# Seven products instead of eight in the last two groups' second products, with a new beginning and a new written order

## The chip, the cores and the metric

The kernel runs on one core of a Trainium2 chip. The metric is the device time of one execution in microseconds (us). TensorE (PE) does the matrix products, VectorE (DVE), ScalarE (ACT) and GpSimd (POOL) the elementwise work, and SyncE (SP) issues nearly all transfers. Each engine takes its instructions in the order in which they stand in its own queue, and waits at one until its semaphores are there.

## The reference

An attention with a decaying state, a gated layer pair and a second layer pair, one behind the other, on 2 x 768 tokens (1536 rows of 512 features):

```python
for t in range(S):                      # per batch and head, D = 64, 8 heads
    state = gamma * state + outer(k[t], v[t])
    y[t] = scale * q[t] @ state
x  = y.reshape(1536, 512)
xn = x / sqrt(mean(x * x, -1) + 1e-06) * rms_g
x2 = (silu(xn @ w_gate) * (xn @ w_val)) @ w_out        # d_ff 1536
h  = x2 @ w_in                                         # d_ff 2048
out = maximum(0.01 * h, h) @ w_out2
```

## The kernel before

The attention runs over 12 chunks of 128 tokens. Its steps have short names in a written order (`ORDER`): `sc` scores, `ds` their decay by the mask (DVE), `kd` decayed keys (DVE for the chunks in `KD`, else ACT), `ou` outer products and `up` the new state, `yi` and `he` the two parts of the output, `sq`, `fa`, `sa`, `to`, `me`, `rs`, `sp`, `xs` the norm, `hi` and `lo` the two parts of the normed rows. Tokens with a colon convert a weight: the weights come as 64-bit numbers (tiles `raw_*`, 512 KB each), ACT and DVE turn one into a float32 tile `wa_*` (`P`, `1` to `4`) and split it into a high and a low part (`H` on ACT, `L` on DVE, tile `w_*`). `M`, `N`, `C` are the first gate and value products. Everything up to `Cv12` stands in this order; behind it, a planner writes the steps and a scheduler sets each engine's order.

Every product is made of three: high by high, high by low, low by high. A step of it is a matmul of 128 x 128 by 128 x 512. The tokens stand in three blocks of 512. The hidden columns come in pieces f of 128: g, v and o are gate, value and output of the first pair of layers (12 pieces, groups of 4, the names of their sums begin with `ao`), i and p input and output of the second (16 pieces, four groups, sums `ap`, kept in `y2acc`). For two pieces and the blocks 1 and 2, the products i (and g, v) are made as seven half products of sums instead of eight (`quad`, steps p1 to p7 into banks X, Y, Z); that takes sums of weights (tiles `w_s*`: four additions on 128 x 256 and two splits on DVE, two on ACT for a pair of pieces) and sums of the rows (`th`, `tl`). Block 0 is made plainly (`whole`).

The second products (`down`, L556) are plain in all blocks: for each piece and block the activated piece is split (`upper`, ACT, tile `gp_*h`; `lower`, DVE L571, tile `gp_*l`), and 12 matmuls add it into four PSUM banks. For p the split activation is the stationary operand and the weight the moving one, so the rows of a bank are tokens. When the four pieces of a group are through, `evac2` adds the four banks to `y2acc` (DVE L633), and in the last group stores them, 128 rows of 2 KB at a time. The last to be stored is block 2.

Seven matmuls on zeros (`warm`) begin PE's work. The small tables are issued by ACT, the rest by SP, in the order of `LOADS` (q, k a chunk's two transfers of 512 KB, m the mask, d the decay of q, w a weight). Transfers share eight completion semaphores in turn (`DMAHW0` to `DMAHW7` in the rows of the order below); one that takes up a semaphore waits for the transfer that had it before.

Of the kernel before, what the change touches and what calls it, by code (L numbers as in the profile page):

```python
# [13 lines left out]
ALU = mybir.AluOpType  # L14
# [10 lines left out]
HOLD = 2  # L25
# [33 lines left out]
def chain_kernel(ctx: ExitStack, tc: tile.TileContext, qk_t, kv, w1, w2, mask, qdec, kdec, sdec, rms_g, ident, out):  # L59
# [18 lines left out]
    scr = ctx.enter_context(tc.tile_pool(name="scr", bufs=5))  # L78
# [16 lines left out]
    expo = const.tile([P, 2], F32, name="expo")  # L95
    state = [const.tile([P, NPAIR, D], F32, name=f"state{i}") for i in range(4)]
# [16 lines left out]
    n_loaded = [0]  # L113

    def load(*items):
        for what in items:
# [6 lines left out]
            elif n == "d":  # L123
                nc.sync.dma_start(out=qdec_sb, in_=qdec)
# [213 lines left out]

    wq = []
    for kinds, fs in groups:  # L340
        for f in fs[::2]:
            for n in kinds:
                wq += [source(n, f), source(n, f + 1)]
                if n in TWICE and f"{n}{f}" not in PLAIN:
                    wq.append((f"s{n}{f}", None))
# [25 lines left out]
    def open_unit():  # L371
# [12 lines left out]
        if src is None:  # L384
# [9 lines left out]
            one, two = slice(0, 2 * P), slice(2 * P, 4 * P)  # L394
# [14 lines left out]

            return key, None, {  # L410
# [171 lines left out]
    def down(gi, f, b):  # L582
# [6 lines left out]
        if b == NB - 1:  # L589
            free(f"{L}{f}")  # L590
# [474 lines left out]
```

## Time and profile before

| | before |
|---|---|
| median of 3 runs | 598.89 us (598.23 to 599.38) |
| the profiled execution | 598.3 us |
| its span | 596.5 us |
| PE, DVE, ACT busy in the span | 583.4, 445.8, 334.2 us |
| mean granted PE clock | 0.994 |

The profile is of one execution; what lies outside its span is 598.3 - 596.5 = 1.8 us. Busy times of PE are modelled: matmuls overlap, so the time from one to the next is read from the chain, and not from the mean duration of one.

### The profile page before, as it was taken

Reading aid. Unit: us, or ns where it says so; the run is one execution under the profiler, and the core shown is the slowest. Engines: PE = TensorE matmul, PEld = TensorE weight load, DVE = VectorE, ACT = ScalarE, POOL = GpSimd, SP = SyncE. Lnnn points to the kernel's source line nnn. Section 1 sums busy time; section 2 is a strip of 40 time slices with the busy share of each in tenths; the row PEclk is TensorE's granted clock in tenths of the full one; section 3 lists DMA queues with packets and bytes.
Section 4 is the critical chain, followed back from the end, with each engine's and each line's share of the span. In section 5 each row is a group of like instructions: output and inputs, shape, how many; then the busy total and the mean of one; then the engine's idle time right before and its main releaser. Section 6 shows DMA issues by size and latency. Waiting matters only on the chain.

```text
span 596.5 us, 8244 instructions
## 1 busy us (share of the span) xinstructions
PE 583.4 (98%) x3147; PEld 482.5 (81%) x3147; DVE 445.8 (75%) x789; ACT 334.2 (56%) x612; POOL 20.7 (3%) x20
## 2 busy tenths in 40 slices
PE   6988999999999999999999999999999999999997
PEld 4977788888888888888888888878888888888885
DVE  3899999998578599599589989875767884631243
ACT  1679756776555465465474666776645474323320
POOL 0442100000000000000000000000000000000000
PEclk8999999999999999999999999999999999999999
DMA  8992321444122223123130211322312210000013
GB/s 301 410 372 73 106 73 35 142 111 128 45 70 72 71 71 88 54 70 110 67 107 0 96 48 35 107 70 73 105 36 70 71 36 1 0 2 0 1 70 141
DMA packets 16310, 52.76 MB, mean 88 GB/s; under 512 B 2448, under 2 KB 2576, under 8 KB 16272
## 3 DMA queue, kind: packets, MB, share of 16 engines
q1 hardware_dynamic: 15408, 52.17, 26.0%
q8 instruction: 24, 0.39, 0.3%
q10 hardware_dynamic: 864, 0.08, 0.1%
q14 instruction: 14, 0.11, 0.1%
HBM read 49.10 MB, written 3.15 MB: 88 GB/s over the span
## 4 chain that ended last, share of the span: by engine, by line
PE 93%; DVE 4%; DMA 2%; issue 1%; ACT 1%; ACTq 0%
PE ap L556 21%; PE ao L556 16%; PE g L526 7%; PE v L526 7%; PE i L526 7%; PE iX L753 7%; PE gX L753 5%; PE vX L753 5%; PE iZ L753 4%; PE gZ L753 2%; PE vZ L753 2%; PE iY L753 2%; PE sc L175 2%; PE y L236 1%; PE vY L753 1%; PE gY L753 1%
## 5 line engine op out<-in xcount | busy, mean ns | idle before, releaser
L556 PE MATMUL ap<-w_p,gp_1h 128*128 128x512 f32 x128 | 39.4, 389 | 0.0
L556 PE MATMUL ap<-w_p,gp_0h 128*128 128x512 f32 x128 | 39.4, 389 | 0.0
L556 PE MATMUL ap<-w_p,gp_2h 128*128 128x512 f32 x128 | 39.4, 389 | 0.0
L571 DVE TENSOR_TENSOR gp_0l<-i,gp_0h 128x512 fp32r<-128x512 f32 x16 | 11.0, 688 | 32.4 <-ACT gp_0h L564 32.4
L526 PE MATMUL g<-xh,w_g 128*128 128x512 f32 x128 | 32.4, 393 | 0.0
L526 PE MATMUL v<-xh,w_v 128*128 128x512 f32 x128 | 31.8, 390 | 0.0
L526 PE MATMUL i<-x2h,w_i 128*128 128x512 f32 x128 | 31.6, 389 | 0.0
L556 PE MATMUL ao<-go_2h,w_o 128*128 128x512 f32 x96 | 31.5, 389 | 0.0
L556 PE MATMUL ao<-go_0h,w_o 128*128 128x512 f32 x96 | 31.5, 389 | 0.0
L633 DVE TENSOR_TENSOR y2acc<-ap,y2acc 128x512 f32<-128x512 f32 x36 | 23.3, 685 | 10.4 <-PE ap L556 10.4
L556 PE MATMUL ao<-go_1h,w_o 128*128 128x512 f32 x96 | 30.5, 389 | 0.0
L526 PEld LDWEIGHTS g<-xh,w_g 128*128 128x128 f32 x128 | 23.7, 188 | 5.5 <-DVE hold L704 0.2
L556 PEld LDWEIGHTS ap<-w_p,gp_0h 128*128 128x128 f32 x128 | 24.0, 188 | 5.0
L556 PEld LDWEIGHTS ap<-w_p,gp_2h 128*128 128x128 f32 x128 | 24.0, 188 | 5.0
L526 PEld LDWEIGHTS i<-x2h,w_i 128*128 128x128 f32 x128 | 24.0, 188 | 5.0
L556 PEld LDWEIGHTS ap<-w_p,gp_1h 128*128 128x128 f32 x128 | 24.0, 188 | 5.0
L526 PEld LDWEIGHTS v<-xh,w_v 128*128 128x128 f32 x128 | 24.0, 188 | 4.9
L556 PE MATMUL ap<-w_p,gp_1l 128*128 128x512 f32 x64 | 25.1, 391 | 0.2 <-DVE gp_1l L571 0.2
L556 PE MATMUL ap<-w_p,gp_0l 128*128 128x512 f32 x64 | 24.9, 389 | 0.0
L556 PE MATMUL ap<-w_p,gp_2l 128*128 128x512 f32 x64 | 24.9, 389 | 0.0
L571 DVE TENSOR_TENSOR gp_2l<-hold,gp_2h 128x512 fp32r<-128x512 f32 x16 | 11.0, 688 | 16.4 <-ACT gp_2h L564 12.4
L564 ACT ACTIVATE gp_2h<-hold 128x512 fp32r<-128x512 f32 x16 | 10.1, 631 | 20.2 <-PE ap L556 20.2
(243 smaller groups left out, 1568.4 us busy)
## 6 DMA issues: line engine op xcount, KB each, us to landing
raw_i<-in_w SPq DMA_DIRECT2D x16, 512.0 KB, 3.7
raw_p<-in_w SPq DMA_DIRECT2D x16, 512.0 KB, 3.7
raw_g<-in_w SPq DMA_DIRECT2D x12, 512.0 KB, 3.6
raw_v<-in_w SPq DMA_DIRECT2D x12, 512.0 KB, 3.7
raw_o<-in_w SPq DMA_DIRECT2D x12, 512.0 KB, 3.6
qkT<-in_qk_t SPq DMA_DIRECT2D x7, 512.0 KB, 8.8
kv<-in_kv SPq DMA_DIRECT2D x7, 512.0 KB, 8.0
out<-y2acc SPq DMA_DIRECT2D x12, 256.0 KB, 2.1
```

Source lines behind the costliest of these rows:

```text
L175: nc.tensor.matmul(out=s["sc"][:, j, a, :], lhsT=k_[r, t], rhs=q_[r, t], start=True, stop=True)
L236: nc.tensor.matmul(out=s["y"][j * D:(j + 1) * D, a * CH:(a + 1) * CH], lhsT=s["kv"][:, 1, e:e + D], rhs=s["a"][:, j, a, :], start=not c % CPB,
L526: nc.tensor.matmul(out=dst, lhsT=lhs, rhs=rhs, start=(n == 0), stop=(n == len(pairs) - 1), skip_group_check=True)
L556: nc.tensor.matmul(out=acc["b"][m], lhsT=lhs, rhs=rhs, start=(start and n == 0), stop=(stop and n == 2))
L564: nc.scalar.activation(out=h, in_=x, func=AF.Copy)
L571: nc.vector.tensor_tensor(out=l, in0=x, in1=h.bitcast(F32), op=ALU.subtract)
L633: nc.vector.tensor_tensor(out=dst, in0=banks[m], in1=dst, op=ALU.add)
L753: nc.tensor.matmul(out=dst, lhsT=lhs, rhs=rhs, start=(start and n == 0), stop=(n == 5), skip_group_check=True)
```

## The change

The last two groups (`SEVEN = 2`) make their second products by seven half products as well. For a pair of pieces, sums of the weights p are formed (`w_sp*`), and sums of the activated pieces of blocks 1 and 2 one behind the other in place (`follow`); each of the seven (`seventh`, key q, numbers 1, 5, 6, 3, 7, 2, 4) is split by `upper` and `lower` like a piece, and goes in 6 matmuls into two banks X or Z. After each of the seven the two banks are added to a part of `y2acc`, while X goes on to gather. Both pairs of a group go through one number before the next; the plain products i of block 0 stand between. In these groups all four i are converted ahead of the p, and block 0's second products follow in the next group, or at the end.

For this the blocks 1 and 2 of all four groups now have features in the rows of a bank: the weight is the stationary operand, read with every second column (`by_quarter`). At the end DVE turns them back in squares of 32 (`transpose`), and 16 transfers of 32 partitions x 16 x 64 numbers store them, in runs of 256 B. Block 0 stays as it was and is stored last.

The beginning: ACT issues one table only, SP the others between the chunks; `turn` is no longer loaded in two broadcasts but made by two small matmuls (`across`). The table of ACT's functions is loaded by a first activation on a constant. Four more matmuls on zeros (`wm1`) stand ahead of `he0`, which now is ahead of `sc1`. `kd1` and `kd2` go to DVE, `kd4` to ACT. The written order is new throughout; a pool of scratch tiles has nine in place of five and two `hold` tiles.

```diff
-HOLD = 2
+SCRATCH = 9
+SEVEN = 2
-LOADS = "q0 k0 m q1 k1 q2 d k2 k3 q3 q4 q5 k4 w w q6 q7 k6 w k8 k7 k5 q8 q9 k9 q10 k10"
+LOADS = "q0 k0 m g s k1 q1 d q2 q3 k2 k3 q4 k4 q5 w w q6 w q7 k6 k8 k7 k5 i q8 q9 k9 q10 k10"
-KD = (0, 3, 4, 6, 7)
+KD = (0, 1, 2, 3, 6, 7)
-sc0 kd0 ts tk ou0 ds0 up0 sc1 kd1 he0 load ds1 sq0 ou1 qs1 xg0 sc2 up1 fa0 kd2 yi1 qs2 ds2 kd3 he1 sa0 qs3 ou2 sq1 sc3
+sc0 kd0 ou0 ds0 tb ts wm1 tk he0 load kd1 up0 sc1 sq0 qs1 xg0 ou1 ds1 qs2 sc2 up1 fa0 yi1 qs3 ds2 he1 kd2 sa0 ou2 kd3
...
+    def keep_warm(c, n=WARM):
+        s = ch.setdefault(c, {})
+        s["sc"] = ps_sc.tile([P, 2, NPAIR, CH], F32, tag="sc", name=f"sc{c}")
+        for _ in range(n):
+            nc.tensor.matmul(out=s["sc"][:, 0], lhsT=warm[:, :P], rhs=warm, start=True, stop=True)
...
+    def by_quarter(w, m):
+        return w.rearrange("p (h c m) -> p h m c", h=2, m=2)[:, m // 2, m % 2]
...
-                terms = (w[:, 0, part], h), (w[:, 0, part], l), (w[:, 1, part], h)
+                wh, wl = (w[:, i, part] if L == "o" else by_quarter(w[:, i, :], m) for i in range(2))
+                terms = (wh, h), (wh, l), (wl, h)
...
-        accumulate(L, gi, f, b, f == fs[0], f == fs[-1], L == "o")
+        accumulate(L, gi, f, b, f == fs[0], f == fs[-1], L == "o" or b > 0)
...
+    def follow(f, n):
+        t = turns[f]
...
+        if n == 1:
+            less(t[0, 1], t[0, 2], t[0, 1])
+            made["q", f, 5] = t[0, 1]
...
+    def seventh(gi, n, f):
...
+        upper(key)
+        lower(key)
+        h, l = parted.pop(key)
+        unit, half, side, start, (b, row) = SIDES[n]
...
+        for m in range(2):
+            wh, wl = (by_quarter(w[:, i, :], 2 * half + m) for i in range(2))
+            for k, (lhs, rhs) in enumerate(((wh, h), (wh, l), (wl, h))):
+                nc.tensor.matmul(
+                    out=acc[side][m],
...
+        for m in range(2):
+            dst = y2[b][:, 2 * row + m, :]
+            nc.vector.tensor_tensor(out=dst, in0=acc[side][m], in1=dst, op=ALU.add)
+        if gi == len(groups) - 1 and LAST[b, row] == n:
+            t = units.tile([P, 16, 32, 2], F32, tag="u", name=f"turned{b}_{row}")
+            for m in range(2):
+                nc.vector.transpose(
...
+            for i in range(4):
+                o = 2 * row * P + i * 64
+                nc.sync.dma_start(
+                    out=out[offs[b]:offs[b] + 512, o:o + 64].rearrange("(j r) d -> r j d", r=32),
+                    in_=t[32 * i:32 * i + 32].rearrange("p j c m -> p j (c m)"),
+                )
```

Three places of the order, before and after. A name's first number is its chunk, piece or group; the last one is a running number. First SP, from the start of the program, before:

```order
L132 DMA qkT0_114<-in_qk_t 128x1024
L134 DMA kv0_115<-in_kv 128x1024
L122 DMA mask_sb_91<-in_mask 128x512 [waits DMAHW0_49]
L122 DMA mask_sb_91<-in_mask 128x512 [waits DMAHW1_49]
L132 DMA qkT1_120<-in_qk_t 128x1024 [waits DMAHW2_49]
L134 DMA kv1_121<-in_kv 128x1024 [waits DMAHW3_49]
L132 DMA qkT2_124<-in_qk_t 128x1024 [waits DMAHW4_49]
L124 DMA qdec_sb_92<-in_qdec 128x512 [waits DMAHW5_49]
L134 DMA kv2_125<-in_kv 128x1024 [waits DMAHW6_49]
```

and of the change:

```order
L135 DMA qkT0_115<-in_qk_t 128x1024
L137 DMA kv0_116<-in_kv 128x1024
L125 DMA mask_sb_91<-in_mask 128x512 x2
L127 DMA g_sb_96<-in_rms_g 128x4
L127 DMA sdecs_94<-in_sdec 128x4
L137 DMA kv1_124<-in_kv 128x1024
L135 DMA qkT1_123<-in_qk_t 128x1024 [waits DMAHW0_49]
L127 DMA qdec_sb_92<-in_qdec 128x512 [waits DMAHW1_49]
L135 DMA qkT2_128<-in_qk_t 128x1024 [waits DMAHW2_49]
```

The scores of chunk 1 (`qkT1`) wait for the third small table of ACT no more but for the first, and the mask for nothing; `kv1` has moved ahead of `qkT1`.

Second PE, behind the scores of chunk 0, before:

```order
L195 MATMUL u0_191<-kv0_115,kd0_181 64x64 [waits DMAHW5_49,DVE_49]
L195 MATMUL u0_191<-kv0_115,kd0_181 64x64 x7
L175 MATMUL sc1_204<-qkT1_120 128x128 [waits DMAHW2_49,PE_49]
L175 MATMUL sc1_204<-qkT1_120 128x128 x7
L236 MATMUL y0_222<-a0_200,kv0_115 64x128 [waits DVE_49] x2
L236 MATMUL y0_222<-a0_200,kv0_115 64x128 x6
```

and of the change (five further matmuls and loads of zeros are left out):

```order
L205 MATMUL u0_186<-kv0_116,kd0_184 64x64 [waits DMAHW2_49,DVE_49]
L205 MATMUL u0_186<-kv0_116,kd0_184 64x64 x7
L1029 MATMUL norm_198<-sdecs_94,one_of_100 128x4 [waits DMAHW6_49]
L1029 MATMUL norm_198<-sdecs_94,one_of_100 128x4
L185 LDWEIGHTS warm_106
L185 MATMUL sc1_204<-warm_106 128x512
...
L185 MATMUL sc1_204<-warm_106 128x512
L246 MATMUL y0_214<-a0_195,kv0_116 64x128 [waits DVE_49] x2
L246 MATMUL y0_214<-a0_195,kv0_116 64x128 x6
L179 MATMUL sc1_204<-qkT1_123 128x128 [waits DMAHW0_49]
L179 MATMUL sc1_204<-qkT1_123 128x128 x7
```

The first heads (`y0`) and the new zeros have moved from behind the scores of chunk 1 into the time ahead of them.

Third DVE in the last group. Before, where the second products of blocks 1 and 2 begin (`gp_12_2l` is the low part of piece 12 for block 2):

```order
L571 TENSOR_TENSOR gp_14_1l_5178<-is1_14_5025,gp_14_1h_5176 128x512 [waits DVE_49,Activation_49]
L772 TENSOR_TENSOR hold15_5125<-iZ14_5094,iu2_14_5073 128x512 [waits PE_49]
L571 TENSOR_TENSOR gp_15_1l_5202<-i15_1_5186,gp_15_1h_5200 128x512 [waits DVE_49,PE_49,Activation_49]
L571 TENSOR_TENSOR gp_12_2l_5218<-hold13_4945,gp_12_2h_5216 128x512 [waits DVE_49,PE_49,Activation_49]
L571 TENSOR_TENSOR gp_13_2l_5242<-hold13_4945,gp_13_2h_5240 128x512 [waits DVE_49,PE_49,Activation_49]
L633 TENSOR_TENSOR y2acc1_3758<-ap_6_1_0_5160,y2acc1_3758 128x512 [waits PE_49]
L633 TENSOR_TENSOR y2acc1_3758<-ap_6_1_1_5161,y2acc1_3758 128x512 [waits PE_49]
L633 TENSOR_TENSOR y2acc1_3758<-ap_6_1_2_5162,y2acc1_3758 128x512 [waits PE_49]
L633 TENSOR_TENSOR y2acc1_3758<-ap_6_1_3_5163,y2acc1_3758 128x512 [waits PE_49]
L571 TENSOR_TENSOR gp_14_2l_5262<-hold15_5125,gp_14_2h_5260 128x512 [waits Activation_49]
```

and of the change, from the end of the first of the seven to the split of the third pair of sums (`gq_14_6l` is the low part of number 6 of the pair 14, 15; `X6`, `Z6` are the banks of group 6):

```order
L725 TENSOR_TENSOR y2acc1_3751<-X6_1_0_5073,y2acc1_3751 128x512 [waits PE_49]
L725 TENSOR_TENSOR y2acc1_3751<-X6_1_1_5074,y2acc1_3751 128x512 [waits PE_49]
L675 TENSOR_TENSOR is1_14_4961<-is5_14_4993,is1_14_4961 128x512 [waits DVE_49]
L422 TENSOR_TENSOR w_sp14_5064<-wa_p14_4917,w_sp14_5064 128x512
L422 TENSOR_TENSOR w_sp15_5065<-wa_p15_4996,w_sp15_5065 128x512 [waits Activation_49]
L602 TENSOR_TENSOR gq_12_6l_5136<-is1_12_4834,gq_12_6h_5134 128x512 [waits Activation_49]
L675 TENSOR_TENSOR iu2_14_4982<-is5_14_4993,iu2_14_4982 128x512
L675 TENSOR_TENSOR is1_12_4834<-i13_1_4950,is1_12_4834 128x512 [waits DVE_49]
L725 TENSOR_TENSOR y2acc2_3891<-Z6_5_0_5126,y2acc2_3891 128x512 [waits PE_49]
L725 TENSOR_TENSOR y2acc2_3891<-Z6_5_1_5127,y2acc2_3891 128x512 [waits PE_49]
L602 TENSOR_TENSOR gq_14_6l_5149<-is1_14_4961,gq_14_6h_5147 128x512 [waits Activation_49]
L602 TENSOR_TENSOR gq_12_3l_5160<-is5_12_4869,gq_12_3h_5158 128x512 [waits Activation_49]
```

Between two splits for PE there now stand additions of sums (L675), splits of weight sums (L422) and twice as many bank additions (L725), where the splits stood alone or behind four additions.

## Rows read from the trace of the kernel before

**Rows 1.** The page: busy us, share of the span and instructions of each engine.
```profile
PE 583.4 (98%) x3147; PEld 482.5 (81%) x3147; DVE 445.8 (75%) x789; ACT 334.2 (56%) x612; POOL 20.7 (3%) x20
```

**Rows 2.** Waits of PE, whole span: us in total, times, longest.
```profile
PE sc L175 <- DMA qkT<-in_qk_t: 3.5, 1, 3.5
...
PE ap L556 <- DVE gp_1l L571: 0.2, 1, 0.2
```

**Rows 3.** Stretches: start:end, length, busy by engine, then PE clock, DMA share, GB/s.
```profile
11.00:14.00 3.00, 3.00 (x26) 2.78 (x28) 0.94 (x1) 1.80 (x4) 0.00 (x0) 0.50 1.03 411
...
17.00:20.00 3.00, 3.00 (x58) 2.70 (x56) 2.33 (x3) 2.20 (x9) 1.94 (x2) 0.99 1.03 411
...
35.00:58.00 23.00, 20.14 (x369) 18.17 (x369) 22.80 (x45) 19.26 (x55) 10.62 (x8) 1.00 0.53 191
58.00:100.00 42.00, 42.00 (x213) 33.95 (x214) 40.77 (x66) 27.13 (x46) 1.80 (x2) 1.00 0.26 78
...
340.00:500.00 160.00, 159.81 (x705) 131.89 (x704) 121.60 (x209) 99.69 (x170) 0.00 (x0) 1.00 0.20 66
500.00:592.00 92.00, 92.00 (x408) 76.20 (x407) 36.84 (x59) 27.93 (x46) 0.00 (x0) 1.00 0.06 23
```

**Rows 4.** The chain that ended last, pieces in order of time: start us, us, what.
```profile
1.17 5.00 DMA turn<-in_sdec
...
6.18 4.63 DMA qkT<-in_qk_t
...
573.75 17.01 PE ap L556 x75
...
590.79 2.73 DVE y2acc L633 x4
```

**Rows 5.** Timeline of the start: start us, us, what, [idle before <- releaser].
```profile
4.29 2.08 PE L175 MATMUL sc<-qkT 64*128 64x128 f32 x16
...
6.04 0.69 DVE L149 TENSOR_TENSOR kd<-kv,kdecs 128x512 f32<-128x512 f32 x1 [4.90 <-DMA kv<-in_kv]
...
10.95 2.08 PE L175 MATMUL sc<-qkT 64*128 64x128 f32 x16 [3.48 <-DMA qkT<-in_qk_t]
...
20.06 1.16 PE L175 MATMUL sc<-qkT 64*128 64x128 f32 x16
...
23.25 0.69 ACT L498 ACTIVATE wa_g<-raw_g 128x512 f32<-128x512 f32 x1 [1.91 <-DMA raw_g<-in_w]
...
26.45 0.42 DVE L428 TENSOR_SCALAR wa_g<-wa_g 128x512 f32<-128x512 f32 x1
...
57.91 2.11 PE L526 MATMUL g<-xh,w_g 128*128 128x512 f32 x8
```

**Rows 6.** Timeline, DVE: four bank additions in a row.
```profile
221.70 2.51 DVE L608 TENSOR_TENSOR x2acc<-ao,x2acc 128x512 f32<-128x512 f32 x4
```

**Rows 7.** Groups by form, DVE, ACT and PE's loads: busy us, mean ns | idle before.
```profile
L437 DVE SCALAR_TENSOR_TENSOR wa_p<-raw_p,wa_p 128x512 int32<-128x512 int32 x16 | 11.0, 689 | 0.4
...
L571 DVE TENSOR_TENSOR gp_0l<-i,gp_0h 128x512 fp32r<-128x512 f32 x16 | 11.0, 688 | 32.4 <-ACT gp_0h L564 32.4
...
L398 DVE TENSOR_TENSOR wa_i<-wa_i 128x256 f32<-128x256 f32 x16 | 6.7, 421 | 0.3
...
L498 ACT ACTIVATE wa_p<-raw_p 128x512 f32<-128x512 f32 x16 | 10.7, 670 | 4.5 <-DVE w_p L453 2.6 <-DVE wa_p L432 1.8
...
L564 ACT ACTIVATE gp_0h<-i 128x512 fp32r<-128x512 f32 x16 | 10.1, 629 | 0.4
...
L556 PEld LDWEIGHTS ap<-w_p,gp_0h 128*128 128x128 f32 x128 | 24.0, 188 | 5.0
```

**Rows 8.** DMA queues from 0 to 15 us, then stores: packets, MB, share of 16 engines.
```profile
q1 hardware_dynamic: 1429, 4.45, 82.9%
q10 hardware_dynamic: 864, 0.08, 4.1%
...
out<-y2acc SPq DMA_DIRECT2D x12, 256.0 KB, 2.1
```

More of the change, by code (lines that the diff above doesn't have):

```diff
@@ L55 @@
+sv2:4 o2:P T3 Nv12 Cv02 Cv12
 """
@@ L721, in used @@
         n, f = key[0], int(key[1:])
-        left[key] = left.get(key, 2 if n in TWICE and key not in PLAIN else NB) - 1
+        left[key] = left.get(key, 2 if doubled(n, f) else NB) - 1
         if not left[key]:
@@ L844, in downs @@
                 return [lambda f=f: put_down((gi, f, b)) for f in fs]
-            fill = downs(groups[gi - 1][1], 2, gi - 1) if gi else []
+            fill = downs(groups[gi - 1][1], 0 if gi - 1 in seven else 2, gi - 1) if gi else []
             first = gi == len(G1)
+            if gi in seven:
+                for f in fs[::2]:
+                    own = [fill.pop(0) for _ in range(2)]
+                    for i7, (keys, step) in enumerate(quad("i", f)):
+                        put(keys, step)
+                        if i7 in BEHIND[2] and own:
+                            own.pop(0)()
+                wholes = [lambda f=f: put((f"i{f}",), lambda: whole("i", f, 0, h, l)) for f in fs]
+                for n, more in zip((1, 5, 6, 3, 7, 2, 4), (1, 0, 1, 0, 1, 0, 1)):
+                    for f in fs[::2]:
+                        order.append(("q", f, n))
+                        keys = (f"p{f}", f"p{f + 1}", f"sp{f}", f"sp{f + 1}")[SIDES[n][0]], "half"
+                        put(keys, lambda n=n, f=f, gi=gi: seventh(gi, n, f))
+                    if more:
+                        wholes.pop(0)()
+                continue
             if first:
@@ L870, in plan @@
                     k = min(-(-len(fill) // (len(ns) - j)), 7)
-                    if n in TWICE and f"{n}{f}" not in PLAIN:
+                    if doubled(n, f):
                         behind = BEHIND[k]
@@ L883, in plan @@
                 d()
-        for d in downs(fs, 2):
+        for d in downs(fs, 0 if gi in seven else 2):
             d()
@@ L904, in pair, with across @@
         return 2 * p, 2 * p + 1
+    def across():
+        nrm["bank"] = acc_bank(3, "norm")
+        for j in range(2):
+            nc.tensor.matmul(
+                out=nrm["bank"][:, j * NPAIR:(j + 1) * NPAIR],
+                lhsT=one_of[:, j:j + 1].to_broadcast([P, P]),
+                rhs=sdecs[:, 0, :, 0],
+                start=True,
+                stop=True,
+            )
     def tables_k():
-        nc.vector.reciprocal(out=turn, in_=turn)
+        nc.vector.reciprocal(out=turn, in_=nrm["bank"][:, :2 * NPAIR].rearrange("p (j a) -> p j a", j=2))
         for i in range(1, CPB - 1):
@@ L968, in chain_kernel @@
     with tc.manual_schedule():
-        wb = ps_sc.tile([P, 2, NPAIR, CH], F32, tag="sc", name="warm_up")
-        for _ in range(WARM):
-            nc.tensor.matmul(out=wb[:, 0], lhsT=warm[:, :P], rhs=warm, start=True, stop=True)
+        keep_warm(0)
         for token in ORDER.split():
```

160 lines of the change are left out of this document (108 added, 52 removed).

## The prediction

> **What bounds the kernel now.** The page comes first: PE is busy for 583.4 us of a span of 596.5, DVE for 445.8 [rows 1]. The list of PE's waits then says how fast it is fed: the longest wait is one of 3.5 us for a transfer near the start, and behind 100 us there is a single one of 0.2 us [rows 2]. The stretches show three stages [rows 3]. To about 58 us the attention runs; from 35 to 58 us DVE is busy for 22.80 of 23 us while PE has gaps, so DVE sets the pace there. From 58 to 100 us both are full. From 100 us on PE is full to the end, DVE in the last 92 us for only 36.84. The chain that ended last confirms it: one transfer behind the other in the first 10.8 us, in the end 75 matmuls in 17.01 us, then four bank additions and the last store [rows 4]. 17.01 / 75 = 0.2268 us is what one matmul costs in this stage. So a matmul taken away behind 58 us is worth 0.227 us as long as PE's operands come in time, and a microsecond won in the attention is worth one if it lasts until PE is full.
>
> **The matmuls taken away.** For two pieces and two blocks the plain second products take 2 x 2 x 12 = 48 matmuls, the seven take 7 x 6 = 42. Two groups with two pairs each: 4 x 6 = 24 fewer, the order of the program has 2316 in place of 2340. 24 x 0.2268 = **5.4 us** less for PE.
>
> **What feeds them.** PE's gain must be paid by DVE. A full instruction lasts 0.688 us [rows 7], but in a row the next starts 0.61 us later: four additions take 2.51 us, (2.51 - 0.685) / 3 = 0.61 [rows 6]. The small ones, 128 x 256, last 0.42 [rows 7]; with the same 0.08 off, 0.34. For a pair of pieces DVE gets 4 small additions and 2 splits of weight sums, 4 additions of activated sums, 3 more splits (7 for 4), and per group 6 more bank additions (14 for 8); at the end 8 transposes. I count the rows of DVE's order against PE's. While PE does the seven of the first such group and the four plain products between them (132 matmuls, 132 x 0.2268 = 29.9 us), DVE has 42 full and 8 small instructions: 42 x 0.61 + 8 x 0.34 = 28.3 us, or with their whole durations 42 x 0.688 + 8 x 0.42 = 32.3. In the last group, from the first of the seven to the end of its last plain product, again 29.9 us of PE, there are 35 full, 2 small and 8 transposes. A transpose has no row; between the 0.42 of a small instruction and twice the 0.688 of a full one I take a full one's, which moves as many numbers. That makes 43 x 0.61 + 2 x 0.34 = 26.9 us, or 30.5 by durations. So DVE just keeps up by the spacing that it shows when it has work waiting, and would lose 2.4 + 0.6 = 3 us by durations. Step by step the tightest place is the one of the third fence of the order: `gq_14_6l` comes some 9.4 us behind the first of the seven, PE wants it at 42 matmuls x 0.2268 = 9.5. ACT, busy for 99.69 us of the 160 from 340 us on [rows 3], has room for the splits that it gets. I charge **0.5 us** for such waits, with 0 and 3 as bounds.
>
> **The weights with every second column.** 192 plain matmuls of the first two groups and 168 of the seven load a weight in this way. A load takes 188 ns [rows 7], and 227 pass from matmul to matmul, so it may become 39 ns longer at no cost. The trace has no strided load on PE. Nearest are the reads of the raw weights, every second word: DVE takes 689 ns for them beside 688 for dense ones, ACT 670 beside 629, 6.5% more [rows 7]; 6.5% of 188 is 12 ns. I take 0. If a load took double, 376 ns, each would cost 376 - 227 = 149 ns, 360 x 0.149 = 54 us; that is the upper bound, and a rival below. The Trainium skill (SBUF — State Buffer, Door 1: The DMA port swizzle) says that memory lines have 16 bytes and that two hits on one suffice for full speed; a stride of two words has two, so by that page it costs nothing, which no run here shows for a load.
>
> **The stores.** The earlier groups' additions stay as they are. The last group's blocks 1 and 2 are stored while PE still works: by the order, 108 matmuls (24.5 us) follow the last one of the first of their four parts and 60 (13.6) that of the last; less 2.7 us for two additions and two transposes, they go out some 22 and some 11 us before PE ends. Block 0, last, takes the same four additions and stores of 2.1 us [rows 8] that block 2 took. So the tail behind the last matmul is worth 0. What may spoil it are 16 x 512 = 8192 runs of 256 B, a rival below.
>
> **The beginning.** Two steps set it now. The scores of chunk 1 wait for their transfer, which was issued at 6.18 us because a small table of ACT held its semaphore [rows 4]; they start at 10.95 and, at a granted clock of 0.50, take 2.08 us, where at full clock the same 16 entries take 1.16 [rows 3, 5]. With the new order qkT0, kv0, the mask and kv1 go out without a wait, qkT1 when ACT's first table has landed. qkT0 landed by 4.29 us, when the first scores start [rows 5]; four transfers of 524 KB at 411 GB/s [rows 3] are 4 x 1.28 us, so qkT1 lands at 9.4, not 10.8: 1.4 us earlier, and so does all that is queued behind it. From 11 us to about 17 us PE runs at 0.50, and at 0.99 behind that [rows 3]. In the gap it now has two small matmuls, four of zeros and the first heads, so I expect its clock to stay up; by the two scores, 1 - 1.16 / 2.08 = 0.44 of those 6 us could go, 2.7 us more, 4.1 in all. The first conversion on DVE starts at 26.45 us [rows 5]. It needs the first raw weight, at 23.25 - 1.4 = 21.9 plus 0.7 for ACT [rows 5]: 22.6. DVE's work ahead of it, the rows of its order by their durations in the trace, is about 14.7 us, or 13.3 with 0.08 off for each; it starts with `kd0` at 6.04 [rows 5] and would be done at 19.3, so it has 3 us to lose in waits. Hence between 1.4 us (only the transfers gain) and 3.9 (26.45 - 22.6). From there to the first dense product (57.91 [rows 5]) both orders give DVE the same work within 0.1 us, and DVE is what that stage waits for, so the gain stays; but the keys of chunks 6 and 7 come only 1.4 us earlier, and DVE may stand before them. I take **3.0 us**, bounds 0 (waits give it back) and 4.1. The zeros and small matmuls lie in PE's wait of 3.48 us ahead of scores 1 [rows 5] and cost nothing; without that cover they would hold up the scores by their own length.
>
> **Sum.** 598.3 of the profiled execution (span 596.5 and 1.8 around it) - 5.4 + 0.5 - 3.0 = 590.4. The median of the runs shown, 598.89, is 0.6 above that execution, so 590.4 + 0.6 = **591.0 us**. The likeliest case's own range is 589.4 to 593.5: the start between 4.1 and 1.5 us, the waits in the seven between 0 and 1.5.
>
> **Rivals.**
> *DVE becomes the bound in the seven.* For it: 28.3 of 29.9 us is 95% full, the sums depend on each other through ACT and DVE in turn, and the four bank additions that wait for PE stand in the same queue. Against: 22.80 of 23 us shows that DVE can be that full [rows 3]. All 3 us: 591.0 - 0.5 + 3 = 593.5, up to 596 if the chains add as much again.
> *The beginning gives only its transfers*, or less: 0 to 1.4 us, for instance because DVE waits for the keys. 592.6 to 594.
> *Strided loads are slow* (the other side). One mechanism: a load of every second column takes over 227 ns. The 5.4 + 3.0 - 0.5 = 7.9 us are eaten up at 7.9 / 360 = 22 ns beyond that, a load of 249 ns, one third longer than now; at double time 591 + 54 = 645. For it: no row shows such a load. Against: DVE's 689 and ACT's 670 ns.
> *The small stores end last.* From 0 to 15 us, the big transfers' packets took 0.829 x 16 x 15 us / 1429 = 139 ns each for 3.1 KB, the tables' 0.041 x 240 / 864 = 11 ns for 93 B [rows 8]. By the former's rate 163 B more are 7 ns, so I take some 20 ns for 256 B, with 11 and 139 as bounds. Each of 16 engines has 512, and some 22 us from the first store to the end of PE: up to 42 ns they are hidden, at 139 they would end 49 us behind. The Trainium skill (DMA: Bandwidth & Descriptors, Specifications) says that transfers under 512 B run below line rate because the engine reads, changes and writes back. If that doubled my 20 ns, an estimate, 40 would still just be hidden; by this page the sum is at the edge.
>
> **How the numbers follow.** A difference of 0.2% (1.2 us) is about what a measurement of this kernel can tell from none. Forecast, 589.4 to 593.5: 0.58. DVE as the bound, 593.5 to 596: 0.12. Little from the beginning, 592.6 to 594: 0.10. More than forecast, below 589.4, if the new order also closes some of PE's 23 - 20.14 = 2.9 us between 35 and 58 us [rows 3]: 0.08. Slow loads, over 600: 0.07. Small stores last, about 599 to 640: 0.03. Both DVE and beginning fail, near 598: 0.02. Faster is the sum of the first four, 0.88; the others make slower 0.09 and same 0.03. The range 587.5 to 595.5 holds the first three, but for a tail of the second, and half of the fourth: about 0.81.
>
> **What would show it.** Right: the last matmuls still at 0.227 us each; PE's list of waits with less than 1 us behind 100 us; the scores of chunk 1 starting near 9.4 us at full clock; the first conversion on DVE at 22.6 to 24 us and the first dense product near 55; loads of 188 ns on the lines of the seven; the transposed stores landing before the last bank additions. Wrong: PE waiting for `gq_*l` on DVE, loads longer than 227 ns, a clock of 0.5 in the first 17 us, or a store from `turned*` as the last end.

## The result and the profile after

| | before | after |
|---|---|---|
| median | 599.13 us (598.23 to 599.58, 4 runs) | 589.69 us (589.66 to 589.85, 4 runs) |
| ratio, 95% interval | | 0.9845 [0.9828, 0.9862] |
| span of the profiled execution | 596.5 us | 587.9 us |

The changed kernel is 1.55% faster. The forecast was 591.0 with a range of 587.5 to 595.5, and its likeliest case reached from 589.4 to 593.5. Of the 8.6 us of span, 4.5 are won before the first dense product, and the sum comes out nearly right for reasons that are partly wrong; the experiments take it apart. The first dense product is PE's first matmul of the gate and value products, with which the steady stage of big matmuls begins.

The page of the changed kernel, the engines' busy time; it answers to [rows 1]:

```profile
PE 579.5 (99%) x3131; PEld 478.4 (81%) x3131; DVE 480.8 (82%) x865; ACT 343.5 (58%) x624; POOL 19.5 (3%) x20
```

PE has 16 records less (24 matmuls fewer of the seven, 8 more at the start) and 3.9 us less to do, DVE 35 us more.

Its waits of PE over the whole span, the longest of them, in us in total, times, longest [rows 2]:

```profile
PE sc L179 <- DVE a L191: 1.3, 1, 1.3
PE sc L185 <- DVE one_of L1016: 1.2, 1, 1.2
PE sc L179 <- DMA qkv<-in_qk_t: 1.0, 2, 0.6
PE norm L1029 <- DMA sdecs<-in_sdec: 0.5, 1, 0.5
PE y L230 <- POOL nr L298: 0.5, 1, 0.5
```

The wait of 3.5 us at the start is gone, and behind 60 us the list has none at all: DVE carries its 35 us more without holding PE up for long. It has little to spare, though. In the stage of the first seven (length, busy PE, PEld, DVE, ACT, POOL, clock, DMA share, GB/s) DVE is busy for 29.24 of 30 us, where its share of the whole span is 82%:

```profile
481.90:511.90 30.00, 30.00 (x131) 24.55 (x130) 29.24 (x52) 16.01 (x27) 0.00 (x0) 1.00 0.11 36
```

The same stretches as in [rows 3], where they bear on it:

```profile
11.00:17.00 6.00, 5.83 (x104) 4.88 (x101) 5.44 (x9) 2.46 (x9) 3.59 (x3) 1.00 1.03 412
...
35.00:58.00 23.00, 22.41 (x344) 19.67 (x341) 22.92 (x42) 21.38 (x60) 8.24 (x7) 1.00 0.47 173
58.00:100.00 42.00, 42.00 (x215) 34.11 (x214) 40.95 (x67) 26.05 (x40) 2.07 (x2) 1.00 0.25 77
...
340.00:500.00 160.00, 160.00 (x700) 132.17 (x699) 122.55 (x211) 96.88 (x166) 0.00 (x0) 1.00 0.16 50
```

PE's granted clock from 11 to 17 us is 1.00 in place of 0.50, and from 35 to 58 us PE is busy for 22.41 us in place of 20.14.

The timeline of the start, the rows that answer to [rows 5] (start us, us, what, in brackets the idle time before and its releaser):

```profile
10.09 1.16 PE L179 MATMUL sc<-qkT 64*128 64x128 f32 x16
...
22.19 0.69 ACT L526 ACTIVATE wa_g<-raw_g 128x512 f32<-128x512 f32 x1 [0.47 <-DMA raw_g<-in_w]
...
23.35 0.42 DVE L456 TENSOR_SCALAR wa_g<-wa_g 128x512 f32<-128x512 f32 x1
...
53.42 0.97 PE L554 MATMUL g<-xh,w_g 128*128 128x512 f32 x3
```

The scores of chunk 1 start 0.9 us earlier, behind the new zeros and the first heads and not behind their transfer, and take 1.16 us; the first weight is on ACT 1.1 us earlier; the first conversion on DVE is 3.1 us earlier; the first dense product 4.5 us (57.91 to 53.42). So 1.4 us more are won behind the first conversion, where the prediction had nothing.

The chain that ended last [rows 4]:

```profile
1.64 4.89 DMA mask_sb<-in_mask
6.55 6.53 DMA qkT<-in_qk_t
13.09 11.63 DMA qkv<-in_qk_t
24.74 9.11 DMA qkv<-in_qk_t
...
53.49 5.69 PE g L554 x24
...
573.30 8.85 PE ap L587 x39
582.16 0.02 issue
582.18 2.73 DVE y2acc L748 x4
```

The last 39 matmuls run at 8.85 / 39 = 0.227 us, and four additions close the kernel as before: from the start of the last row to the end it is 5.7 us in both spans. The chain at the start leads through transfers to 34 us; the experiments show that this isn't what sets the time there.

Last, PE's loads of weights by form, and the stores from the transposed tiles:

```profile
L587 PEld LDWEIGHTS ap<-w_p,gp_0h 128*128 128x128 f32 x128 | 24.0, 188 | 5.0
...
L587 PEld LDWEIGHTS ap<-gp_1h,w_p 128*128 128x128 f32 x64 | 12.4, 193 | 2.6
```

```profile
out<-turned SPq DMA_DIRECT2D x16, 128.0 KB, 2.5
```

The second row of loads has the kernel's `by_quarter` blocks, with every second column: 193 ns in place of 188. The 16 stores take 2.5 us from issue to landing.

### The profile page after: what moved, and what is told of

Its sections match the earlier page's. It is cut to its first block, busy times and chain, and to the rows that moved or that the text cites. A ratio compares the mean times of both kernels' runs of the same rounds, so it can differ in the third digit from the quotient of the medians.

```text
span 587.9 us, 8302 instructions
## 1 busy us (share of the span) xinstructions
PE 579.5 (99%) x3131; PEld 478.4 (81%) x3131; DVE 480.8 (82%) x865; ACT 343.5 (58%) x624; POOL 19.5 (3%) x20
## 3 DMA queue, kind: packets, MB, share of 16 engines
HBM read 49.09 MB, written 3.15 MB: 89 GB/s over the span
## 4 chain that ended last, share of the span: by engine, by line
PE 93%; DMA 5%; DVE 0%; issue 0%; SPq 0%
PE ao L587 17%; PE ap L587 15%; PE g L554 7%; PE v L554 7%; PE iX L858 7%; PE i L554 7%; PE vX L858 5%; PE gX L858 5%; PE X L706 4%; PE iZ L858 4%; DMA qkv<-in_qk_t 4%; PE Z L706 3%; PE vZ L858 2%; PE gZ L858 2%; PE iY L858 2%; PE vY L858 1%
## 5 line engine op out<-in xcount | busy, mean ns | idle before, releaser
L587 PE MATMUL ap<-gp_2h,w_p 128*128 128x512 f32 x64 | 21.4, 394 | 0.0
L587 PEld LDWEIGHTS ao<-go_0h,w_o 128*128 128x128 f32 x96 | 18.0, 188 | 3.7
L587 PEld LDWEIGHTS ao<-go_1h,w_o 128*128 128x128 f32 x96 | 18.0, 188 | 3.7
L587 PEld LDWEIGHTS ao<-go_2h,w_o 128*128 128x128 f32 x96 | 18.0, 188 | 3.7
L587 PE MATMUL ap<-gp_1h,w_p 128*128 128x512 f32 x64 | 20.9, 394 | 0.0
L801 ACT ACTIVATE i<-i 128x512 f32<-128x512 f32 x16 | 9.5, 596 | 18.7 <-PE i L554 18.7
L858 PE MATMUL iX<-th,w_si 128*128 128x512 f32 x64 | 19.8, 390 | 0.0
L858 PE MATMUL iZ<-x2h,w_si 128*128 128x512 f32 x64 | 19.7, 389 | 0.0
L587 PE MATMUL ao<-go_0l,w_o 128*128 128x512 f32 x48 | 18.7, 389 | 0.0
L587 PE MATMUL ao<-go_1l,w_o 128*128 128x512 f32 x48 | 18.7, 389 | 0.0
```

The costliest lines, as they stand in the source:

```text
L587: nc.tensor.matmul(out=acc["b"][m], lhsT=lhs, rhs=rhs, start=(start and n == 0), stop=(stop and n == 2))
L801: nc.scalar.activation(out=a, in_=x, func=AF.Prelu, alpha=0.01)
L858: nc.tensor.matmul(out=dst, lhsT=lhs, rhs=rhs, start=(start and n == 0), stop=(n == 5), skip_group_check=True)
```

## The experiments

Times are medians; "before" moved between 598.95 and 599.53 from one set of runs to the next, so experiments are compared with each other and with the changed kernel (589.7).

**Seven or eight products.** Two kernels keep the beginning, the nine scratch tiles and the written order, and make one group or none by seven.

```diff
-SEVEN = 2
+SEVEN = 0        # e_seven1: 1
-        accumulate(L, gi, f, b, f == fs[0], f == fs[-1], L == "o" or b > 0)
+        accumulate(L, gi, f, b, f == fs[0], f == fs[-1], L == "o" or (SEVEN and b > 0))   # e_seven0 only
```

> The changed kernel with no group by seven (plain second products and plain stores, as before): only the beginning, the pool of 9 scratch tiles and the new order are left. Theory, the beginning is worth 4.5 us and the 1.2 us that vanish between 100 and 400 us come with the order or the pool: 599.1 - 5.7 = 593.4. Rival, these 1.2 us come with the seven: 594.6. By the terms of the prediction (3.0): 596.1.

> The changed kernel with only the last group by seven. Theory, each group is worth its 12 matmuls, 2.7 us, and the strided loads cost what they do with two groups (372 in place of 360): 589.7 + 2.7 + 0.1 = 592.5. Rival, DVE is the bound in one of the two groups and eats its gain: 589.7 to 590.5 if it is the first, over 594 if the last.

Measured: e_seven0 592.63 us (ratio 0.9895 [0.9881, 0.9909]), e_seven1 592.47 (0.9893 [0.9879, 0.9908]). The second seven is worth 592.47 - 589.69 = 2.8 us, as 12 matmuls should. The first one with all that comes with it (the transposed layout of blocks 1 and 2) is worth 0.2: its 2.7 us are eaten by 372 strided loads, as the next experiment shows. And all the rest of the change is worth more than was thought of in the prediction, and more than in the theory ahead of this run: 598.95 - 592.63 = 6.3 us; by spans 596.5 - 590.7 = 5.8. Not all of this is won at the beginning: up to the first dense product it is 57.91 - 53.50 = 4.4 us, and from there to the end, where both kernels have the same matmuls, 538.6 us became 537.2. [rows 2] lists a single wait of 0.2 us there; the rest of these 1.4 us lies in gaps between PE's matmuls that are too short for that list.

**Loads of every second column.** The host lays the columns of w2's second part out so that a block of 128 lies side by side; the last additions of block 0 put the columns back. The line that reads the block:

```diff
-        return w.rearrange("p (h c m) -> p h m c", h=2, m=2)[:, m // 2, m % 2]
+        return w[:, m * P:(m + 1) * P]
```

> The changed kernel with weight blocks that lie side by side in place of every second column (the host lays the columns of w2's second part out that way; the last four additions of block 0 put them back in order). Theory, strided loads cost 6.7 ns for each of 360 matmuls: -2.4 us, 587.3; loads of 188 ns on the lines of the seven and 2.72 us for 12 matmuls. Rival, these matmuls are slower for another reason (the weight is what is loaded): loads stay at 193 ns and the time at 589.7.

Measured: 587.50 us (0.9808 [0.9794, 0.9822]), 2.2 less than the changed kernel, and 2.4 less span (585.5). One line of the seven in the changed kernel (minimum, median and maximum in ns), then the same in e_dense:

```profile
L706 PEld LDWEIGHTS X<-gq_1h,w_p x16: 193/193/194, 481.9 to 545.0; 128*128 128x128 f32 x16
L706 PE MATMUL X<-gq_1h,w_p x16: 394/394/395, 482.1 to 545.2; 128*128 128x512 f32 x16
```

```profile
L706 PEld LDWEIGHTS X<-gq_1h,w_p x16: 187/188/188, 480.4 to 543.0; 128*128 128x128 f32 x16
L706 PE MATMUL X<-gq_1h,w_p x16: 389/389/389, 480.6 to 543.2; 128*128 128x512 f32 x16
```

The load is 5 ns longer, the matmul too, and in the chain 12 matmuls take 2.80 us in place of 2.72. 0.08 / 12 = 6.7 ns, times 360 is 2.4 us. The rival falls: with dense blocks the difference is gone, and weights were what is loaded in both kernels. So the 39 ns between a load of 188 and the next matmul at 227 aren't free time into which a longer load could grow. What is left in e_dense are four places in the seven where a matmul starts 0.07 us late behind a `gq_*l`; with still shorter ones PE's matmuls behind 340 us start some 0.4 us later in all than 0.227 us apart would give, where e_seven0 has 0.03.

**The stores.** Dense blocks again, but now the transposed tile holds 32 columns of one bank side by side, and goes out in runs of 128 B:

```diff
-            t = units.tile([P, 16, 32, 2], F32, tag="u", name=f"turned{b}_{row}")
+            t = units.tile([P, 16, 2, 32], F32, tag="u", name=f"turned{b}_{row}")
...
-                o = 2 * row * P + i * 64
-                nc.sync.dma_start(
+                for m in range(2):
+                    o = (2 * row + m) * P + i * 32
+                    nc.sync.dma_start(
```

> The changed kernel with weight blocks side by side, and the last transposed results stored in runs of 128 B in place of 256 (32 stores, 16384 runs). Theory, some 22 ns for a run on each of 16 engines, 1024 x 22 = 22.5 us in all, of which the later half starts some 11 us ahead of the end: just hidden, 587.5 as e_dense. Rival, runs cost the same for half the bytes and the stores end last: the time grows by up to 10 us, and a store from a turned tile is the last to land.

Measured: 587.50 us (0.9806 [0.9794, 0.9822]), the same as e_dense, and the chain ends with PE and four additions as there. So twice as many runs are still hidden behind PE's work, and the rival of the small stores had room to spare.

**Which part of the beginning.** Three kernels undo one part each of the changed kernel: the order of the large transfers, the zeros, the place of the small tables. The last one, e_tables, also loads `turn` by two broadcasts again in place of the two small matmuls, and leaves out the early load of ACT's functions. Where the diff has a comment, it names the kernel.

```diff
-LOADS = "q0 k0 m g s k1 q1 d q2 q3 k2 k3 q4 k4 q5 w w q6 w q7 k6 k8 k7 k5 i q8 q9 k9 q10 k10"
+LOADS = "q0 k0 m g s q1 k1 q2 d k2 k3 q3 q4 q5 k4 w w q6 q7 k6 w k8 k7 k5 i q8 q9 k9 q10 k10"   # e_loads
...
-sc0 kd0 ou0 ds0 tb ts wm1 tk he0
+sc0 kd0 ou0 ds0 tb ts tk he0                                                              # e_no_zeros
...
-    nc.scalar.activation(out=ready, in_=expo, func=AF.Silu)                               # e_tables
+    for j in range(2):
+        nc.scalar.dma_start(out=turn[:, j], in_=sdec[j * D:j * D + 1, :, 0].to_broadcast([P, NPAIR]))
+    nc.scalar.dma_start(out=sdecs[:, 0], in_=sdec)      # rms_g and ident likewise, g s i taken out of LOADS
```

> The changed kernel with the order of before for the transfers of queries, keys and weights (the small tables stay where they now stand). Theory, the chain that leads through transfers to 34 us is real, and the written order wants its own order of transfers: 591 to 593, with a wait of PE or DVE for a transfer of over 1 us between 10 and 40 us. Rival, DVE sets the beginning: 589.7 to 590.2.

> The changed kernel without the four matmuls of zeros ahead of the scores of chunk 1. Theory, they hold PE's clock: granted clock 0.5 in the stretch from 10 to 17 us and 2.7 us of the beginning gone: 592.4. Rival, the first heads and the two small matmuls hold it: clock 1.00 from 8 to 17 us and 589.7. Second rival, the clock falls but transfers set the time to 34 us anyway: 589.7 to 590.3 at a clock of 0.5.

> The changed kernel (589.7) with the small tables issued by ACT again, the two spread tables loaded in place of the two small matmuls, and no early table load for ACT's functions; order of transfers and written order as changed. Theory, the tables on ACT's queue delay the transfers behind them by the 1.4 us of the prediction: 591.1. Rival, with the new order DVE has enough else to do: 589.7 to 590.0. Second rival, the zeros and scores find their bank later and the delay grows: over 592.

Measured: e_loads 589.60 us, e_no_zeros 590.11 (0.9853 [0.9839, 0.9868]), e_tables 591.88 (591.14 to 596.80; its profiled execution 591.14, span 589.3).

The order of the large transfers is worth nothing. So, in this written order, the chain that leads through transfers to 34 us doesn't set the time, since another order of them ends at the same time.

The zeros are worth 0.4 us at most. They aren't what keeps PE's clock: the stretch from 8 to 12 us in e_no_zeros is at 1.00 without them. And that clock isn't what the time hangs on. In another run (e_hold, below, the zeros in place) the same stretch was granted 0.57, and its first dense product still starts at 53.50 us, as in e_seven0, which is the nearest kernel to it. No run in the new order has the clock down as long as before had it, to 17 us. But the executions of before itself speak against a price: two of the 32 that ran beside the experiments had a mean granted clock of 1.000, so they can't have stood at 0.50 for 6 of 596 us, which alone makes 0.995. Their spans are 596.6 and 596.8 us, where the 32 have a median of 597.1: some 0.4 us and not 2.7. The stretch in e_no_zeros, then in e_hold (length, busy PE, PEld, DVE, ACT, POOL, clock, DMA share, GB/s):

```profile
8.00:12.00 4.00, 2.90 (x50) 2.40 (x49) 2.52 (x10) 1.63 (x5) 0.99 (x1) 1.00 1.00 395
```

```profile
8.00:12.00 4.00, 4.00 (x26) 2.40 (x26) 2.30 (x11) 0.00 (x0) 0.90 (x1) 0.57 1.02 414
```

The tables are worth what the prediction gave to the transfers, by the profiled execution: in e_tables the chain begins as before, with a transfer of chunk 1's queries behind a small table, and its first dense product starts at 54.79 us, 1.4 later; the span is 1.4 longer. By medians it is 2.2 us, and the six executions lie 5.7 us apart, with the profiled one the fastest; what the others lose wasn't followed. That 1.4 is right is borne out by e_old_order (below), which has the tables' new place and the old written order: its first dense product starts at 56.65 us, 1.3 ahead of before.

```profile
1.18 4.95 DMA turn<-in_sdec
6.53 4.41 DMA qkT<-in_qk_t
```

**The tiles and the written order.** Both on the kernel without the seven (592.63 us, span 590.7). e_hold brings back the five scratch tiles and the two doubled tiles for block 2; e_old_order the written order of before, with its choice of chunks in `KD` and without the zeros.

```diff
-SCRATCH = 9                                                   # e_hold
+SCRATCH = 5
...
+        if key[1] == 2:
+            return hold(key)
```

```diff
-KD = (0, 1, 2, 3, 6, 7)                                       # e_old_order
+KD = (0, 3, 4, 6, 7)
-sc0 kd0 ou0 ds0 tb ts wm1 tk he0 load kd1 up0 sc1 sq0 qs1 xg0 ou1 ds1 qs2 sc2 up1 fa0 yi1 qs3 ds2 he1 kd2 sa0 ou2 kd3
+sc0 kd0 tb ts tk ou0 ds0 up0 sc1 kd1 he0 load ds1 sq0 ou1 qs1 xg0 sc2 up1 fa0 kd2 yi1 qs2 ds2 kd3 he1 sa0 qs3 ou2 sq1 sc3
...
```

> The kernel without the seven (e_seven0, 592.6) with 5 scratch tiles and the two doubled tiles for block 2 back in place of 9 scratch tiles. Theory, the tiles are what held PE up between 100 and 400 us before: 592.6 + 1.2 = 593.8, and the loss of about half a microsecond near 391 us is back. Rival, the order of the beginning moved these losses: 592.6, no loss there.

> The kernel without the seven (592.6) with the written order of before (and before's choice of chunks whose keys DVE scales), without the zeros; table loads, order of transfers and the nine scratch tiles as in the changed kernel. Theory, transfers and table loads give the 1.4 us that the prediction gave them, and the written order the other 3.1 of 4.5: 592.6 + 3.1 = 595.7. Rival, the transfers alone give all: 592.6 to 593.2.

Measured: e_hold 593.04 us (0.9897 [0.9879, 0.9914]), e_old_order 596.63 (0.9956 [0.994, 0.9971]). The tiles are worth 0.4 us and not 1.2. The written order, with `KD` and the zeros (which alone are worth 0.4 at most), is worth 4.0 us, more than all else at the beginning: the first dense product starts at 56.65 us with the old order and at 53.50 with the new one. The first dense product of e_old_order, then of e_seven0:

```profile
56.65 0.97 PE L554 MATMUL g<-xh,w_g 128*128 128x512 f32 x3
```

```profile
53.50 2.11 PE L554 MATMUL g<-xh,w_g 128*128 128x512 f32 x8
```

PE's short wait for `gp_1l` near 391 us [rows 2] is there in e_old_order too and gone with the new order, so it belongs to the order as well. PE's clock has no part in it that could be seen: in e_old_order's profiled execution it is down at 0.50 from 11 to 14 us (mean 0.994, 596.57 us), and two executions at a mean of 1.000 took 596.45 and 596.68.

**Why the order is worth so much.** DVE is what this stage waits for: from 35 to 58 us it is busy for 22.80 of 23 us [rows 3]. In the kernel before, DVE and POOL up to 42 us (each engine's timeline; here the engine is the third column):

```profile
40.35 0.46 DVE L263 TENSOR_TENSOR sq<-sq 128x256 f32<-128x256 f32 x1
40.73 1.76 DVE L446 CUSTOM_DVE_ANT_0 wa_v<-wa_v,wb_v 128x1024 uint16<-128x1024 uint16 x1
42.42 0.41 DVE L212 TENSOR_TENSOR state<-u,sdecs 128x256 f32<-128x256 f32 x1
```

```profile
40.49 1.46 POOL L165 TENSOR_TENSOR qs<-qkT,qdec_sb 128x512 f32<-128x512 f32 x1
```

The conversion at 40.73 lasts 1.76 us where its like lasts 0.68. It begins while POOL scales a chunk's queries (`qs`), and ends behind POOL. There are two more of this kind, so that the three are 1.07 to 1.08 us too long each: a sum at 19.71 (its like takes 0.28) and a conversion at 27.45 (0.42, as the one at 26.45 in [rows 5]).

```profile
19.71 1.36 DVE L268 TENSOR_TENSOR ss<-sq 128x128 f32<-128x128 f32 x1
27.45 1.50 DVE L428 TENSOR_SCALAR wa_g<-wa_g 128x512 f32<-128x512 f32 x1
```

With smaller ones DVE's instructions up to the first dense product are 3.65 us longer than their like elsewhere, 2.2 us of this behind the first conversion. It can go the other way: the first of two scalings at 37.21 us begins while DVE is at work, DVE's next instructions take their usual time, and POOL takes 3.32 us for two scalings, where two take 2.50 at 14.20 us.

```profile
37.21 3.32 POOL L165 TENSOR_TENSOR qs<-qkv,qdec_sb 128x512 f32<-128x512 f32 x2
37.48 0.67 DVE L437 SCALAR_TENSOR_TENSOR wa_v<-raw_v,wa_v 128x512 int32<-128x512 int32 x1
```

In the order of the changed kernel two scalings meet DVE near 35 us, and cost nothing:

```profile
34.89 0.69 DVE L465 SCALAR_TENSOR_TENSOR wa_v<-raw_v,wa_v 128x512 int32<-128x512 int32 x1
35.29 2.66 POOL L168 TENSOR_TENSOR qs<-qkv,qdec_sb 128x512 f32<-128x512 f32 x2 [6.37 <-PE sc L179]
35.50 2.35 DVE L191 TENSOR_TENSOR a<-sc,mask_sb 128x1024 f32<-128x1024 f32 x2
37.76 0.73 DVE L474 CUSTOM_DVE_ANT_0 wa_v<-wa_v,wb_v 128x1024 uint16<-128x1024 uint16 x1
```

Two scalings on POOL run beside two decays of scores, whose one input lies in PSUM, and these take 2.35 us as everywhere. Up to its first dense product the changed kernel has 0.48 us of such lengthening, e_old_order 3.43. The Trainium skill (SBUF — State Buffer, Who interferes with whom) has the rule: GpSimd's reads of SBUF and a VectorE instruction with both inputs there (or a `tensor_scalar` in a two-port mode) want the same port, and whoever comes second stands until the other is done. These rows agree: the two conversions and the sum that stood have their inputs in SBUF, the decays that did not have one in PSUM; and at 37.21 us it was POOL that came second and stood.

That the rows look so doesn't show that the time hangs on it, and not all of it does. In e_hold an `sq` at 17.60 us stands for 1.07 us, 1.80 with the others, against 0.43 in e_seven0, and both reach the first dense product at 53.50 us: this one, ahead of the first conversion, cost nothing.

```profile
17.60 1.49 DVE L273 TENSOR_TENSOR sq<-sq 128x256 f32<-128x256 f32 x1
```

So the scalings went to DVE in both orders of the kernel without the seven, which leaves only the short `nr` steps on POOL:

```diff
-            nc.gpsimd.tensor_tensor(out=s["qs"], in0=by_pair(s["qkT"][:, 0, :]), in1=qdec_sb, op=ALU.mult)
+            nc.vector.tensor_tensor(out=s["qs"], in0=by_pair(s["qkT"][:, 0, :]), in1=qdec_sb, op=ALU.mult)
```

> e_old_order (written order of before, no group by seven, 596.6) with the ten scalings of queries on DVE in place of POOL, so that nothing of POOL's meets DVE. Theory, a DVE instruction with both inputs in SBUF that begins while POOL runs such a scaling stands until POOL is done, and before's order has 3.4 us of this up to the first dense product, the new order 0.4: DVE pays 10 x 0.61 = 6.1 us, or 3.7 if four of them fall into its idle time ahead of 26 us, and gets 3.4 back: 596.9 to 599.3; and the distance to e_new_dve shrinks from 4.0 to 1.0 us. Rival, the collisions are hidden and the order itself is worth 4.0: 600.3 to 602.7, distance 4.0.

> e_seven0 (new written order, no group by seven, 592.6) with the ten scalings of queries on DVE. Theory: DVE pays 3.7 to 6.1 us and gets 0.4 back: 595.9 to 598.3, 1.0 us below e_old_dve. Rival: the same 595.9 to 598.7, but 4.0 us below e_old_dve.

Measured: e_old_dve 596.33 us (0.9953 [0.9938, 0.9968]), e_new_dve 594.86 (0.9932 [0.9916, 0.9948]). With the scalings on DVE the old order gets 0.3 us faster, although DVE has ten instructions more to do, and the new one 2.2 slower. No DVE instruction of either is longer than its like up to the first dense product, which starts at 56.06 and 55.45 us (e_new_dve's profiled execution is 0.7 us above its median). The two starts, e_old_dve first:

```profile
56.06 1.42 PE L554 MATMUL g<-xh,w_g 128*128 128x512 f32 x5
```

```profile
55.45 2.11 PE L554 MATMUL g<-xh,w_g 128*128 128x512 f32 x8
```

The distance between the orders falls from 4.0 to 1.5 us, at the first dense product from 3.15 to 0.6. It goes where it should: from the first conversion to the first dense product e_old_order takes 32.1 us and e_seven0 30.2, with the scalings on DVE they take 30.9 and 30.8. So some 2.5 of the order's 4.0 us are these collisions. e_old_dve came out 0.6 and e_new_dve 1.0 us below the lower end of their expectations, so the price of a scaling on DVE was put too high; where this lies wasn't followed. In e_new_dve POOL still meets DVE, and stands: an `nr` that begins at 64.20 us, DVE at work, takes 3.34 us where another takes 0.69, and PE waits 0.9 us for it.

```profile
64.20 3.34 POOL L298 TENSOR_TENSOR nr<-na,expo 128x2 f32<-128x2 f32 x1 [11.75 <-DVE na L294]
```

**Further by seven.** Dense blocks, and a third group by seven:

```diff
-SEVEN = 2
+SEVEN = 3
```

> The kernel with blocks that lie side by side (e_dense, 587.5) and three groups by seven in place of two. Theory, 12 matmuls less are worth 2.7 us as long as DVE keeps up: 584.8. Rival, DVE, full to 93% in the seven by the prediction's count, falls behind in the third: 586 to 588, with PE waiting for split sums.

Measured: 585.08 us (0.9763 [0.9742, 0.9784]), 2.4 below e_dense and 4.6 below the changed kernel: the fastest of all. The third group is worth 2.4 us of the 2.7 of its 12 matmuls. DVE is now busy for 495.1 us of 583.4, and PE still has no listed wait behind 60 us; but in the stages of the seven DVE is full, as in the second row, and PE's matmuls behind 340 us start 0.7 us later in all than 0.227 us apart would give. So DVE just keeps up there.

```profile
PE 574.3 (98%) x3119; PEld 473.7 (81%) x3119; DVE 495.1 (85%) x897; ACT 347.3 (60%) x634; POOL 19.5 (3%) x20
```

```profile
418.00:448.00 30.00, 30.00 (x134) 24.56 (x133) 29.59 (x54) 16.90 (x30) 0.00 (x0) 1.00 0.16 53
```

## Why the prediction was right, and where its terms were not

| term | predicted | measured, by spans | from |
|---|---|---|---|
| 24 matmuls fewer | -5.4 | -5.2 | e_seven0 590.7 to e_dense 585.5, waits included |
| waits of PE on DVE in the seven | +0.5 | in the row above, under 0.4 | none listed behind 60 us |
| strided loads | 0 | +2.4 | e_dense 585.5 to the changed kernel 587.9 |
| the beginning, with the order and the tiles | -3.0 | -5.8 | before 596.5 to e_seven0 590.7 |
| sum | -7.9 | -8.6 | |

The mechanism of the seven held: matmuls at 0.227 us with dense blocks (0.233 with strided ones), DVE about as full as counted (95% counted, 29.24 of 30 us measured) and late by some 0.07 us at a time, at most. Of the two counts of DVE's time the lower one, by the spacing of a full queue, was the right one.

Two terms were mis-sized, by +2.4 and -2.8 us, and their errors met: that the sum came within 1.3 us of the measured median is luck to that extent.

*"I take 0"* for the strided loads failed. The step behind it said that a load may become 39 ns longer at no cost, because 227 ns pass from matmul to matmul. The load became 5 ns longer and each matmul cost 6.7. The estimate of 12 ns for the load, from ACT's strided reads, was about as far off as the 0 taken for it; what failed is that a longer load costs nothing. The rule cited there (the Trainium skill, SBUF — State Buffer, Door 1: The DMA port swizzle: two words of a line suffice) gives nothing for this stride; the measurement differs from it by 2.2 us of the median (2.4 of the span), and decides. The rival of slow loads needed 249 ns to turn the result; they have 193.

*"I take 3.0 us"* for the beginning came out as 5.8, beyond its upper bound of 4.1; 4.4 of this is there at the first dense product. Of the two parts of that bound the first held in size: the tables out of ACT's queue are worth 1.4 us (e_tables), though the scores of chunk 1, by which the 1.4 was reckoned, start at 10.09 us and not near 9.4. The second, 2.7 us from a clock that stays up, has no support: the clock did stay up, but a run with the clock down from 8 to 12 us reached the first dense product at the same time as one without, two executions of before at full clock are some 0.4 us shorter than the median, and the zeros that were to hold the clock are worth 0.4 us at most. What came in its place is the written order, 3.9 us of span. The step that failed is "both orders give DVE the same work within 0.1 us": they do in rows of the order, but not in what these rows cost, because the durations from the trace of before held 3.65 us of standing behind POOL, 2.2 of it behind the first conversion, that no row shows as a wait. That is why the first conversion came in the range given (23.35 for 22.6 to 24) and the first dense product 1.6 us ahead of the 55 forecast. The remaining 0.4 us of the 5.8 are the scratch tiles, which the prediction had at nothing.

The case named "more than forecast" asked for a time below 589.4, which didn't come, by 0.3 us; the condition that it named did come. It spoke of PE's gaps between 35 and 58 us [rows 3], and these closed from 2.9 to 0.6 us, part of it because dense products now fill the last 4.5 us of that stretch: in the 22.9 us ahead of the first dense product PE's gaps went from 2.9 to 1.0. That they follow from DVE's standing, and aren't a cause of their own, is an inference from DVE being full there.

Not settled: of the order's 4.0 us, about 1.5 remain when the scalings are off POOL. 0.6 of that is there at the first dense product; the rest comes later, and one piece of it is the short wait near 391 us, where two matmuls of before start 0.57 and 0.34 us behind the one ahead of them in place of 0.227, 0.46 us in all.

## What to carry to other kernels

Before costing an order of work by durations from a trace, look for single instructions that last longer than their like: such a surplus is a wait that no list of waits shows, and reordering can remove it or bring it; it costs only where that engine sets the pace. Where PE's weights change from dense to strided, count a few ns on every matmul (6.7 here), even when the load seems to have room. And a forecast that hits its number can hold two errors of opposite sign; kernels that undo one part each tell that for the price of a few runs.

## What the runs showed of the hardware

- Three DVE instructions that began during a scaling on POOL, their inputs in SBUF, ended behind it, and took 1.07 to 1.08 us more than their like. DVE's list of waits has none of it; with an input in PSUM there was no lengthening (2.35 us for two decays beside 2.66 us of POOL). Where POOL began second, POOL took longer: 3.32 us for two scalings in place of 2.50, and 3.34 for an `nr` in place of 0.69.
- PE's load of a 128x128 float32 block with every second column took 193 ns for 188, and 12 matmuls 2.80 us for 2.72, although load and matmul overlap.
- A 32x32-wise transpose of 128x512 float32 on DVE takes as long as an addition of that size, 685 ns in the median of eight.
- Stores in runs of 128 B and of 256 B were both hidden behind PE's work here: a store of 64 KB landed after 1.9 us in the median, one of 128 KB after 2.5.
